# One run of score matmuls for a unit's two tiles, in a fused attention and expert-layer kernel with a planned order

## The chip, the cores and the metric

The kernel runs on one core of a Trainium2 chip. The metric is the device time of one execution in microseconds (us), the median over several runs. A core has five engines that matter here: TensorE (PE; its weight loads are listed as PEld), VectorE (DVE), ScalarE (ACT), GpSimd (POOL) and SyncE (SP), whose queue issues all the DMA transfers of this kernel (SPq in the rows). Each engine works through its own instructions strictly in order and waits on semaphores for the others.

## What is computed

Attention over 8 batches, 8 heads, 576 positions and 64 dimensions, with keys and values averaged over groups of 8 positions (72 pooled keys per head), followed by a dense layer with two weight matrices and a gate on the 4608 resulting rows of 512.

```python
k_p = k.reshape(B, H, Sp, pool, D).mean(axis=3)
v_p = v.reshape(B, H, Sp, pool, D).mean(axis=3)
scores = scale * np.matmul(q, k_p.transpose(0, 1, 3, 2))
scores = scores - np.max(scores, axis=-1, keepdims=True)
attn = np.exp(scores)
attn = attn / (np.sum(attn, axis=-1, keepdims=True) + 1e-09)
x = np.matmul(attn, v_p)            # then (B, S, H*D), as 4608 x 512
h = x @ w_in                        # 512 -> 2048
sp = np.maximum(h, 0.0) + np.log1p(np.exp(-np.abs(h)))
out = (h * erf(sp)) @ w_out         # 2048 -> 512
```

## The kernel before, in words

The 4608 rows are cut into nine chunks of 512. Chunk 0 is computed plainly (stage 0), while the weights are converted from their 64-bit form into two limbs each and written back to HBM. The other eight chunks are taken in pairs (stages 1 to 4) with a Strassen-like scheme of seven products instead of eight. Each product of two matrices is three matmuls of limbs (`three`, line 807 in every row of a large matmul).

Attention is done by `unit`. A unit is 256 rows, that is two tiles of 128; there are 18 units, two of them in chunk 0 and 16 in the others. For each tile `softmax_tile` does this: SP loads the query tile (`raw`, line 632, buffer kind "q" with two buffers for the 16 later units and "q0" with four for chunk 0). TensorE computes the scores into two PSUM banks (`scores`, line 641): 4 head pairs, two key sources, two halves, so 16 matmuls that each use a quarter (64x64) of the array. The profile counts each of these twice, as 32. DVE takes the row maximum of each bank (line 649) and subtracts it (line 665), and with that the bank is read out. ACT takes a sigmoid that stands for the exponential (line 669), DVE sums and inverts (lines 671, 676), DVE or POOL scales (line 679), `copy` sets aside a corner (`bb`). TensorE transposes (lines 686 and 687, five full-array matmuls per tile), ACT or DVE moves the result out, and `part` multiplies with the values (line 734 on quarters, line 740 on halves of the array).

The order of all this is not the source order. Every step is recorded as an `Op` with an engine, an assumed cost, a priority and the buffers that it holds. `Program.order` then places the operations with a list scheduler (`once`). The table MOVES is a list of accepted random shifts of the priorities, so other numbers there mean another order everywhere. Two things in the scheduler matter here. Operations with `step=True` (scores and values, the ones on parts of the array) are charged 200 ns where they follow other work, and are preferred next to each other. Where the planner expects TensorE to be idle (before its time 57 us, or for over 1.2 us), it puts in *fillers*, matmuls on constants that write a bank about to be used (line 1115):

```python
if new and (start < FILL or idle > LONG_IDLE):
    begin = max(free["PE"], 4800.0 if not free["PE"] else 0.0, slots["bank"][0][0])
    out.extend([(self.filler, new[0])] * int((start - begin - MARGIN) / 107))
```

PSUM has eight banks. CAPS limits how many of them each kind may hold at a time: "h" (first layer) 6, "o" (second layer) 4, "att" (attention) 4. An operation is only placed when all its banks are free at once.

Of the kernel before, what the change touches and what calls it, by code (L numbers as in the profile page):

```python
# [25 lines left out]
P = 128  # L26
# [14 lines left out]
PASSES, UNIT = 8, 5100.0  # L41
SPREAD, REACH, SPAN = (300.0, 1000.0, 3000.0), (6e3, 20e3, 60e3), 860e3
MOVES = (
# [7 lines left out]
T0, T0_STEP = -10.5, 1.5  # L51
VAL_R = 3.5
KEYS, KEYS_R, KEYS_S = -5.5, 0.5, -1.0
# [8 lines left out]
ON_ACT = ()  # L62
ON_FIRST = (False, False, False, False)
CAPS = {"fk": 2 * KEPT, "g": 32, "x": 28, "xr": 11, "w": 14, "ws": 10, "w0": 36, "gl": 12, "gz": 16, "t": 6, "f": 3, "q": 2, "q0": 4, "f0": 14, "v": 3, "k": 5, "vm": 1, "low": 2, "sw": 8,
        "h": 6, "o": 4, "att": 4, "cv": 3, "dl": 3, "p1": 8}
SLACK, SLACK_SP, BIAS = 30, 400, 1000
FILL, MARGIN, LONG_IDLE = 57000.0, 300, 1200.0
DGE = 1200
# [322 lines left out]
def moe_attention(ctx: ExitStack, tc: tile.TileContext, cst, qa, kl, vl, wi, wo, out):  # L391
# [16 lines left out]
    op = pr.op  # L408

    def buf(home, shape, dtype=F32):  # L410
        return Buf(small, [P] + shape, dtype, home, home)

    def place(kind, dtype=F32, shape=(512,), name=None):
        return Buf(space, [P, *shape], dtype, "u", name or kind, [kind])

    def bank(kind):
        return Buf(banks, [P, 512], F32, "bank", kind, [kind])
# [195 lines left out]
    def unit(ck, u0, tiles, parts, moment):  # L613

        n_all = 256
        first = ck == 0
# [6 lines left out]
        def softmax_tile(at, r):  # L623
# [4 lines left out]
            rows = [(keys_of[b], e - u0 - at) for e in (u0 + at, u0 + at + 64) for b, off, n, _ in parts if off <= e < off + n]  # L628
            raw = place("q0" if first else "q", F32, (NP, P))
            s = Probs(None, None, None, "s", "s")  # L630
            m, z, bb = buf("m", [H]), buf("z", [H]), buf("bb", [2, 2, NP, SP - 64])
# [3 lines left out]
            pss = [bank("att") for _ in range(2)]  # L635

            def scores():
# [3 lines left out]
                            nc.tensor.matmul(pss[x].ap[r0:r0 + 64, SP * p:SP * p + SP], raw.ap[h:h + 64, p, r0:r0 + 64],  # L641
                                             ks.ap[h:h + 64, p], start=p == 0, stop=True, skip_group_check=True)

            op("PE", 550, r, scores, [raw, *(ks for ks, _ in rows)], pss, [s, m, z],
               turn="q", step=True)
            for g, ps in enumerate(pss):
                pv = lambda ps=ps: ps.ap[:T, :4 * SP].rearrange("p (h k) -> p h k", k=SP)
                gs = slice(4 * g, 4 * g + 4)
# [52 lines left out]
            if k + T == n_all:  # L701
# [3 lines left out]
                    etb.ap[:, 1], f32(etb.ap[:, 0]), c[:, C_MA:C_MA + 1], pb.ap[:, :n_all], ALU.mult, ALU.add),  # L705
                   [pb, (etb, 0)], [(etb, 1)])

        for i in range(tiles):
            softmax_tile(P * i, moment(u0 // P + i))
        plain = ck == 0  # L710
        if ck not in xt:
            if plain:
# [358 lines left out]
    jobs = {}  # L1071
    for ck, u0, tiles, parts in units():

        def moment(t, ck=ck):
            if ck == 0:
                return T0 + T0_STEP * t
            s = (ck + 1) // 2
            at = (t + 4 * ((ck - 1) % 2)) / 8
            return (FIRST - 13 + 9 * at) if s == 1 else start(s) - EARLY[s] + at * (EARLY[s] - READY)

        jobs.setdefault((ck + 1) // 2, []).append((ck, u0, tiles, parts, moment))
    for j in jobs[0]:
        unit(*j)
# [6 lines left out]
    for s in range(1, NC // 2 + 1):  # L1090
        for j in jobs[s]:
            unit(*j)
        x = sides(s, start(s))
# [61 lines left out]
```

## Time and profile before

| what | value |
|---|---|
| runs | 796.21, 796.25, 798.11 us; median 796.25 |
| the profiled execution, its own time | 796.99 us |
| its span in the profile | 795.2 us |
| TensorE busy | 782.6 us, 98% |
| VectorE, ScalarE, GpSimd busy | 81%, 68%, 53% |
| granted TensorE clock, mean | 0.999 |
| bytes moved | 209.78 MB, 264 GB/s |

The span is what the engines' records cover; the profiled execution's own time is 1.79 us more, and that execution is 0.74 us above the median. Busy time is the union of an engine's instructions. Because matmuls are pipelined, the time that a run of matmuls really takes is best read as the distance from its start to the start of what follows on TensorE.

### The profile page before, as it was taken

The numbers are of one execution on the slowest core, as the hardware profiler recorded it, in microseconds if no ns is written. First come the engines' busy times: TensorE is split into PE (matmuls) and PEld (weight loads), VectorE is DVE, ScalarE is ACT, GpSimd is POOL, SyncE is SP. The second block draws the span as 40 slices with busy tenths as digits, with TensorE's granted clock in tenths as the row PEclk, the third lists the DMA queues.
The fourth block names the chain that finished last, engine by engine and source line by source line (L and its number), as shares of the span: only waits on it lengthen the run. The fifth ranks groups of instructions, "written<-read, shape, count | busy, mean of one in ns | idle before, by whom it ended". The sixth has DMA issues, their size and how long they took to land.

```text
span 795.2 us, 15470 instructions
## 1 busy us (share of the span) xinstructions
PE 782.6 (98%) x5288; PEld 671.9 (85%) x5288; DVE 640.5 (81%) x1099; ACT 537.7 (68%) x835; POOL 419.7 (53%) x419
## 2 busy tenths in 40 slices
PE   8999999999999999999999999999999999999998
PEld 6888788877888888888888888888888888888887
DVE  6999886877797887589889979888899976667982
ACT  3999984689865642588775644878856437988730
POOL 4989943479778710275772330775554104561710
PEclk9999999999999999999999999999999999999999
DMA  9989999999999799985485689933745869458551
GB/s 335 347 287 342 364 341 374 332 343 358 291 357 331 245 354 353 367 295 165 149 286 163 204 274 341 339 96 118 247 164 159 277 220 338 145 162 262 186 185 54
DMA packets 126446, 209.78 MB, mean 264 GB/s; under 512 B 12448, under 2 KB 44576, under 8 KB 126368
## 3 DMA queue, kind: packets, MB, share of 16 engines
q1 hardware_dynamic: 126368, 208.79, 76.6%
q8 instruction: 43, 0.70, 0.4%
q14 instruction: 35, 0.29, 0.1%
HBM read 161.55 MB, written 47.19 MB: 263 GB/s over the span
## 4 chain that ended last, share of the span: by engine, by line
PE 85%; ACT 3%; DMA 2%; DVE 2%; SPq 1%; issue 1%; POOL 0%; DVEq 0%; ACTq 0%
PE o L807 42%; PE h L807 35%; PE att L641 2%; PE att L734 2%; PE att L686 2%; PE att L740 2%; DMA ws<-ws 1%; DMA q<-qa 1%; SPq L519 1%; DMA wi<-w 1%; ACT d L826 0%; ACT L826 0%; PE att L687 0%; ACT low L496 0%; ACT cv L492 0%
## 5 line engine op out<-in xcount | busy, mean ns | idle before, releaser
L807 PE MATMUL o<-gl,w 128*128 128x512 f32 x1536 | 340.2, 381 | 0.0
L807 PEld LDWEIGHTS o<-gl,w 128*128 128x128 f32 x1536 | 287.8, 189 | 40.9 <-DVE gl L450 0.2
L807 PE MATMUL h<-x,w 128*128 128x512 f32 (+1 forms) x1392 | 298.9, 374 | 1.2 <-DVE t L914 1.1
L807 PEld LDWEIGHTS h<-x,w 128*128 128x128 f32 x1392 | 253.8, 189 | 36.5 <-DVE t L914 1.8
L834 POOL TENSOR_TENSOR g<-d,g 128x512 f32<-128x512 f32 x79 | 101.9, 1309 | 96.9 <-ACT d L830 95.7
L438 ACT ACTIVATE gl<-g 128x512 fp32r<-128x512 f32 x181 | 107.0, 623 | 44.7 <-DVE g L977 21.8
L450 DVE TENSOR_TENSOR gl<-g,gl 128x512 fp32r<-128x512 f32 x152 | 115.8, 792 | 5.0 <-ACT gl L438 3.3
L450 POOL TENSOR_TENSOR gl<-g,gl 128x512 fp32r<-128x512 f32 x56 | 77.2, 1390 | 54.2 <-ACT gl L438 38.4
L914 DVE TENSOR_TENSOR g<-t,h 128x512 f32<-128x512 f32 x96 | 65.5, 684 | 28.6 <-PE h L807 27.7
L977 POOL TENSOR_TENSOR g<-g 128x512 f32<-128x512 f32 x37 | 60.4, 1632 | 28.8 <-DVE g L977 13.2
L830 ACT ACTIVATE d<-d 128x1024 f32<-128x1024 f32 x72 | 73.5, 1051 | 0.4
L826 ACT ACT_TABLE_LOAD x44 | 56.5, 1283 | 18.6 <-PE h L807 10.9
L914 DVE TENSOR_TENSOR t<-t,h 128x512 f32<-128x512 f32 x57 | 39.1, 686 | 28.9 <-PE h L807 24.4
L826 ACT ACTIVATE d<-g 128x512 f32<-128x512 f32 x103 | 59.2, 622 | 4.6 <-DVE g L914 4.5
L830 ACT ACT_TABLE_LOAD x39 | 50.0, 1283 | 0.7
L438 ACT ACTIVATE x<-xr 128x512 fp32r<-128x512 f32 (+2 forms) x55 | 28.9, 551 | 28.9 <-DVE xr L781 24.3
L669 ACT ACTIVATE s<-s,cst 128x576 f32<-128x576 f32 x36 | 27.6, 772 | 25.0 <-DVE s L665 24.8
L977 DVE TENSOR_TENSOR g<-g 128x512 f32<-128x512 f32 x59 | 44.1, 760 | 0.4
L807 PE MATMUL h<-x,ws 128*128 128x512 f32 x192 | 43.6, 380 | 0.0
L807 PEld LDWEIGHTS h<-x,ws 128*128 128x128 f32 x192 | 36.1, 189 | 5.1
L649 DVE TENSOR_REDUCE m<-att 128x4 f32<-128x288 f32 x72 | 30.1, 444 | 4.9 <-PE att L641 4.8
L439 POOL TENSOR_SCALAR bb<-s 128x64 f32<-128x64 f32 x40 | 10.5, 273 | 43.6 <-DVE s L679 22.6
(107 smaller groups left out, 959.4 us busy)
## 6 DMA issues: line engine op xcount, KB each, us to landing
w<-ws SPq DMA_DIRECT2D x192, 256.0 KB, 4.8
w<-wo SPq DMA_DIRECT2D x128, 256.0 KB, 3.8
w<-wi SPq DMA_DIRECT2D x96, 256.0 KB, 5.2
ws<-ws SPq DMA_DIRECT2D x64, 256.0 KB, 4.6
v<-vl SPq DMA_DIRECT2D x40, 256.0 KB, 5.2
q<-qa SPq DMA_DIRECT2D x36, 256.0 KB, 5.1
out<-f SPq DMA_DIRECT2D x35, 256.0 KB, 2.3
k<-kl SPq DMA_DIRECT2D x32, 256.0 KB, 5.2
```

What stands on the lines that cost most here:

```text
L438: op("ACT", act(n), prio, lambda: nc.scalar.activation(dst(), src(), AF.Copy, scale=scale), *access, turn=turn, alt=("POOL", 0.833 * n + 1 ...
L450: both(True, dve(n), gps(n), prio + 0.1, lambda e: e.tensor_sub(lo(), src(), f32(hi())), reads + [hikey], [lokey])
L641: nc.tensor.matmul(pss[x].ap[r0:r0 + 64, SP * p:SP * p + SP], raw.ap[h:h + 64, p, r0:r0 + 64], ks.ap[h:h + 64, p], start=p == 0, stop=True ...
L649: op("DVE", dve(4 * SP), r + 0.4, lambda pv=pv, gs=gs: nc.vector.tensor_reduce(m.ap[:T, gs], pv(), AX.X, ALU.max), [ps], [(m, g)])
L669: op("ACT", act(H * SP) + 93, r + 0.8, lambda: nc.scalar.activation(s.keys[:T], s.keys[:T], AF.Sigmoid, bias=bias[0][:T], scale=1.0 / 64.0 ...
L686: nc.tensor.transpose(pa.ap[:, P * p:P * p + T], s.keys[:T, p, SP - 64:SP + 64], ident[:T, :T])
L807: nc.tensor.matmul(o, u, v, start=first and q == 0, stop=last and q == 2, skip_group_check=True)
L826: nc.scalar.activation(y(k), hs[k][0].ap, AF.Softplus)
L830: op("ACT", act(1024), prio + 0.2, lambda k=k: nc.scalar.activation(ys[k].ap, ys[k].ap, AF.Erf), own[2 * k:2 * k + 2], own[2 * k:2 * k + 2 ...
L834: both(True, dve(512), gps(512), prio + 0.3, lambda e, k=k, h=h: e.tensor_mul(h.ap, y(k), h.ap), [own[k], h], [h])
L914: op("DVE", dve(512), prio, lambda: nc.vector.tensor_add(dst.ap, u.ap, o.ap), [u, o], [dst])
L977: both(True, dve(512), gps(512), prio, lambda e: e.tensor_sub(out.ap, u.ap, v.ap), [u, v], [out])
```

## The change

The scores of the two tiles of a unit become one operation, except in chunk 0. `softmax_tile` turns into a generator: up to the scores it prepares the tile and hands out its function, inputs, banks and buffers; `unit` collects both tiles' share, records one PE operation for both (32 listed matmuls, 64 in the trace, in four PSUM banks that are all held at once), and then lets the generators run on. "att" may hold six banks instead of four. MOVES is another table with 87 entries instead of 81, of which one row is shown.

```diff
@@ MOVES
-    12000002, 12000013, 12000018, 12000022, 12000032, 12000045, 12000050, 12000120, 12000129, 12000132, 12000145, 12000165,
+    1000000, 1000005, 1000015, 1000023, 1000026, 1000038, 1000043, 1000052, 1000067, 1000085, 1000114, 1000137,
...
@@ CAPS
-        "h": 6, "o": 4, "att": 4, "cv": 3, "dl": 3, "p1": 8}
+        "h": 6, "o": 4, "att": 6, "cv": 3, "dl": 3, "p1": 8}
@@ softmax_tile
-            op("PE", 550, r, scores, [raw, *(ks for ks, _ in rows)], pss, [s, m, z],
-               turn="q", step=True)
+            reads, holds = [raw, *(ks for ks, _ in rows)], [s, m, z]
+            if first:
+                op("PE", 550, r, scores, reads, pss, holds, turn="q", step=True)
+            yield r, scores, reads, pss, holds
@@ unit
+        softmax = []
         for i in range(tiles):
-            softmax_tile(P * i, moment(u0 // P + i))
+            softmax.append(softmax_tile(P * i, moment(u0 // P + i)))
+
+        jobs = [next(t) for t in softmax]
+        if not first:
+            op("PE", 480 * tiles + 70, jobs[0][0], lambda: [j[1]() for j in jobs], *([x for j in jobs for x in j[n]] for n in (2, 3, 4)),
+               turn="q", step=True)
+        for t in softmax:
+            next(t, None)
```

How the order moves is shown at three places, in the program's order and without times. A row is a line of the source, an operation, what it writes and reads, its shape, and how often it stands in a row. Below the edit the changed kernel's lines are higher: 642 for 641, 689 and 690 for 686 and 687, 745 and 751 for 734 and 740, 818 for 807, 1126 for 1115.

First, TensorE where chunk 0 is done and stage 1 begins. Before, the last fillers, the last values of chunks 1 and 2, then the first layer of stage 1 without a break:

```order
L1115 LDWEIGHTS cst
L1115 MATMUL att<-cst 128x256
L734 MATMUL att<-et,vs 64x256 x8
L740 MATMUL att<-etb,vb 128x256 x8
L807 MATMUL h<-x,w 128x512 x66
L807 MATMUL h<-x,ws 128x512 x18
```

In the changed kernel, the last of 29 fillers, values, and only here the last joined scores of chunks 1 and 2, with the transposes of the unit before directly behind them:

```order
L1126 LDWEIGHTS cst
L1126 MATMUL att<-cst 128x256
L745 MATMUL att<-et,vs 64x256 x8
L751 MATMUL att<-etb,vb 128x256 x8
L642 MATMUL att<-ks,q 64x72 x32
L689 MATMUL att<-cst,s_72 128x128 x4
L690 MATMUL att<-cst,bb 128x128
L689 MATMUL att<-cst,s_71 128x128 x4
L690 MATMUL att<-cst,bb 128x128
```

and 31 rows further on the last values of chunk 2, 42 matmuls of the first layer, and then 43 fillers, of which the first is shown:

```order
L818 MATMUL h<-x,w 128x512 x12
L745 MATMUL att<-et,vs 64x256 x8
L751 MATMUL att<-etb,vb 128x256 x8
L818 MATMUL h<-x,w 128x512 x42
L1126 LDWEIGHTS cst
L1126 MATMUL h<-cst 128x256
```

The attention of the second unit of chunk 2 has moved behind the end of chunk 0, into the beginning of stage 1.

Second, TensorE in stage 2, as an example of the steady part. Before:

```order
L734 MATMUL att<-et,vs 64x256 x8
L740 MATMUL att<-etb,vb 128x256 x8
L641 MATMUL att<-ks,q 64x72 x16
L807 MATMUL h<-x,w 128x512 x24
L641 MATMUL att<-ks,q 64x72 x32
L807 MATMUL h<-x,w 128x512 x36
```

Changed:

```order
L818 MATMUL h<-x,w 128x512 x24
L642 MATMUL att<-ks,q 64x72 x32
L745 MATMUL att<-et,vs 64x256 x8
L751 MATMUL att<-etb,vb 128x256 x8
L818 MATMUL h<-x,w 128x512 x54
```

A run of 16 listed matmuls has become one of 32. Over the whole program there were 18 runs of 16 and 9 of 32 and there are now 2 of 16 and 17 of 32; the stretches of matmuls on parts of the array (runs of scores and values that touch each other count as one stretch) go from 35 to 30, and the fillers from 209 (66 of them behind the first matmul of the first layer) to 246 (98).

Third, SP's queue where the last queries for chunks 1 and 2 are loaded. Before, between two weight loads of chunk 0:

```order
L489 DMA d<-wo 128x1024 x3
L519 DMA wi_88<-w_882 256x1x256
L632 DMA q<-qa 128x512
L516 DMA wf_105<-f_868 128x512
L519 DMA wi_96<-w_842 128x256
L519 DMA wi_96<-w_864 128x256
L516 DMA wf_113<-f_985 128x512
L632 DMA q<-qa 128x512
L519 DMA wi_89<-w_889 256x1x256
```

These are the sixth and seventh of the eight "q" loads of chunks 1 and 2. They stand apart, and the eighth too stands ahead of every store of a result. In the changed kernel the third unit's pair and the fourth unit's two loads:

```order
L633 DMA q<-qa 128x512 x2
L528 DMA wo_174<-w_1419 256x1x256
L528 DMA wo_174<-w_1491 256x1x256
L530 DMA wf_127<-f_1564 128x512
L530 DMA wf_118<-f_1415 128x512
L528 DMA wo_167<-w_1412 256x1x256
L956 DMA out<-f 128x512 x2
L633 DMA q<-qa 128x512
L956 DMA out<-f 128x512 x2
L633 DMA q<-qa 128x512
```

The fourth unit's queries now stand behind the stores of chunk 0's results.

## Rows read from the trace of the kernel before

**Rows 1.** The page: busy times; the granted clock in 40 slices

```profile
PE 782.6 (98%) x5288; PEld 671.9 (85%) x5288; DVE 640.5 (81%) x1099; ACT 537.7 (68%) x835; POOL 419.7 (53%) x419
...
PEclk9999999999999999999999999999999999999999
```

**Rows 2.** Waits of PE: who waited for whom: us in total, times, longest

```profile
PE att L1115 <- DMA cst<-cst: 2.7, 1, 2.7
PE o L1115 <- DVE f L500: 1.6, 1, 1.6
PE att L641 <- DMA q<-qa: 1.4, 1, 1.4
PE h L807 <- DVE t L914: 1.1, 1, 1.1
PE att L641 <- DVE ks L582: 0.7, 1, 0.7
PE att L686 <- DVE f L500: 0.6, 1, 0.6
```

**Rows 3.** Timeline of PE, stage 1: start us, us, engine, line, operation, count

```profile
212.71 0.73 PE L641 MATMUL att<-ks,q 64*64 64x72 f32 x32
213.37 2.86 PE L807 MATMUL h<-x,ws 128*128 128x512 f32 x12
216.06 1.46 PE L807 MATMUL h<-x,w 128*128 128x512 f32 x6
217.36 1.46 PE L807 MATMUL o<-gl,w 128*128 128x512 f32 x6
...
221.24 6.64 PE L807 MATMUL o<-gl,w 128*128 128x512 f32 x30
227.81 1.23 PE L641 MATMUL att<-ks,q 64*64 64x72 f32 x64
228.97 11.92 PE L807 MATMUL o<-gl,w 128*128 128x512 f32 x54
240.73 0.60 PE L686 MATMUL att<-cst,s 128*128 128x128 f32 x4
...
241.74 1.54 PE L807 MATMUL o<-gl,w 128*128 128x512 f32 x6
```

**Rows 4.** The same timeline, values and scores with nothing between them

```profile
254.72 1.09 PE L734 MATMUL att<-et,vs 64*64 64x256 f32 x16
255.75 0.74 PE L740 MATMUL att<-etb,vb 64*128 64x256 f32 x8
256.42 0.73 PE L641 MATMUL att<-ks,q 64*64 64x72 f32 x32
257.08 2.86 PE L807 MATMUL o<-gl,w 128*128 128x512 f32 x12
```

**Rows 5.** The same timeline, a block of fillers in stage 1

```profile
201.02 2.68 PE L1115 MATMUL h<-cst 128*128 128x256 bf16 x23
203.46 2.84 PE L807 MATMUL h<-x,ws 128*128 128x512 f32 x12
```

**Rows 6.** Timeline of DVE: the four banks of one long run are read

```profile
124.82 0.96 DVE L649 TENSOR_REDUCE m<-att 128x4 f32<-128x288 f32 x2 [3.25 <-PE att L641]
...
127.16 0.81 DVE L665 TENSOR_TENSOR s<-att,m 128x288 f32<-128x288 f32 x2
```

**Rows 7.** Timeline of PE: that long run of scores itself

```profile
124.04 1.23 PE L641 MATMUL att<-ks,q 64*64 64x72 f32 x64
125.20 2.86 PE L807 MATMUL o<-gl,w 128*128 128x512 f32 x12
```

**Rows 8.** Timeline of PE at the start: scores of the first tile, its transposes

```profile
7.93 0.73 PE L641 MATMUL att<-ks,q 64*64 64x72 f32 x32 [0.72 <-DVE ks L582]
...
16.53 0.60 PE L686 MATMUL att<-cst,s 128*128 128x128 f32 x4
```

**Rows 9.** Loads of the query tile (line 632): all 36, issue to landing

```profile
DMA to landing us min/median/max: 2.6/5.1/7.0
```

13 rows, old and new, of the table MOVES are left out of this document.

## The prediction

> **What bounds the kernel now.** I read the busy times first, then TensorE's waits, then its timeline around attention. TensorE is busy for 782.6 of 795.2 us, and its granted clock stands at the top level (2.4 GHz) in all 40 slices [rows 1]. So nothing off TensorE counts unless it makes TensorE wait, and each instruction on it counts in full. What it waits for is short [rows 2]: 2.7 us for the constants before its first matmul, which the change does not touch, and then 1.6, 1.4, 1.1, 0.7 and 0.6 us, together 5.4 us. The lines in these waits belong to the load of the first keys, the weight conversion of stage 0 (line 500), the products of stage 1 (line 914) and one load of queries. The busy time also holds fillers, matmuls that stand where the planner expected TensorE to be idle. So a different order shows its price in three places: work on parts of the array, fillers, and waits that no filler covers.
>
> **The price of a run of scores.** Six large matmuls take 1.30 us from start to start, so one takes 0.2165 [rows 3]. A short run (32 in the trace) lasts from 212.71 to 213.37, 0.66 us; a long one (64) from 227.81 to 228.97, 1.16 us. So two short runs made into one save 2 x 0.66 - 1.16 = 0.16 us in themselves. There is a cost at either edge too. The 30 large matmuls ahead of the long run take 6.57 us instead of 30 x 0.2165 = 6.49, so entering costs 0.08 to 0.09; the 12 behind the short run take 2.69 instead of 2.60, so leaving costs 0.09 to 0.10. I take 0.19 for a stretch with both edges. Between two kinds of such work there is no edge: behind a product on halves of the array the short run again takes 0.66 us, from 256.42 to 257.08 [rows 4].
>
> **The sum.** In the program's order 18 short and 9 long runs become 2 short and 17 long: eight pairs are joined, 8 x 0.16 = 1.3 us less. (The other eight units outside chunk 0 had their two tiles next to each other already.) Stretches fall from 35 to 30: 5 x 0.19, about 1.0 us less. Fillers rise from 209 to 246. In stage 1, 23 of them take 201.02 to 203.46, 0.106 us each [rows 5], so 37 more add 3.9 us. That is certain, because a filler runs whether or not there was anything to wait for. With all of the 5.4 us of waits taken out the span would be 795.2 - 5.4 - 1.3 - 1.0 + 3.9 = 791.4 us, plus the waits of the new order.
>
> The Trainium skill (TensorEngine Tiling (Array Packing), Key Properties) says that a change of tiling mode drains the engine, a change between tiles of one mode does not. By that rule each change would cost: 106 of them become 95, and at half an edge pair each (0.095) this gives 1.0 us, with nothing for the joining itself, and the sum would be 1.3 us higher. The trace disagrees in part: a change from halves to quarters shows no edge [rows 4], and a long run costs less than two short ones, so I keep my count.
>
> **The new waits.** There are five, none of which the trace shows as it will be; each is bounded from its nearest row.
>
> - *Start.* Nine more fillers stand ahead of the first scores, 9 x 0.106 = 0.95 us, more than the 0.7 us waited there [rows 2]. Nothing is left.
> - *Weight conversion.* 1.6 and 0.6 us were waited here. In the new order large matmuls of chunk 0 come earlier and the attention of chunks 1 and 2 later. That takes attention work off ACT and DVE ahead of the conversions, but TensorE also arrives sooner. Between 0 and 2.2 us; I take 0.4, since less work stands ahead of each conversion.
> - *Fourth unit's queries.* With two "q" buffers these loads must wait until the third unit's run has ended, and SP issues them behind the stores of chunk 0's results. From the last matmul of chunk 0 TensorE has ten transposes (240.73 to 241.74, 1.0 us [rows 3]), 29 fillers (3.1 us) and the values of one part (254.72 to 256.42, 1.7 us [rows 4]), 5.8 us. A query load takes 2.6 to 7.0 us to land, 5.1 in the median [rows 9], and it must first wait for the last results to be copied out of PSUM. At the median that is about on time. Between 0 and 2.5 us; I take 0.5, near the median. Behind the waiting run on TensorE stand the third unit's transposes and the whole first layer of stage 1; behind the loads on SP stand stores of converted weights, which nobody needs soon.
> - *Fourth unit's chain.* From its scores to its transposes the order leaves 1.16 us for the run, 1.0 for ten transposes, 10 fillers (1.1), twice six large matmuls (2.6) and the values of two parts, which are half as wide as the part in [rows 4] and so at most 1.7 us each: at most 9.2, and near 8 if they take little over a microsecond. At the start of the kernel the way from scores to transposes took 7.93 to 16.53, 8.6 us [rows 8]. Between 0 and 1.0; I take 0.3.
> - *Stage 1's products and first queries.* The 1.1 us for line 914 may return; the 43 fillers ahead of the products give DVE time to catch up, so 0.4 of 0 to 1.1. The 1.4 us for a query tile becomes a wait for two tiles: 0 to 2.8. The second load stands 17 places behind the first on SP, but TensorE arrives later than before, so I take 1.0.
>
> Together 0.4 + 0.5 + 0.3 + 0.4 + 1.0 = 2.6 us, and the span comes to 794.0. All of this is made against one execution, whose own time is 1.79 us above its span and 0.74 above the median, so the median lies 1.05 us above the span: **795.0 us**, a gain of 1.2 us, 0.15%. About 0.3%, or 2.4 us, is what a measurement of this kernel can tell from no change, so this counts as *same*.
>
> **The rivals.**
>
> *Faster: the fillers cover everything.* The planner put its fillers exactly where it saw TensorE idle; if it sees the new order well, waits all but vanish. With 0.5 us left the span is 791.9 and the median 793.0. For it: no block of fillers in stage 1 is followed by a wait of its own, and three of the five old waits lie at conversions and queries, places that the new order moves. Against it: the planner was no less exact before and 5.4 us were left over.
>
> *Slower: four banks at once.* A joined run holds four of eight banks until DVE has read them. In the trace DVE starts on such a run at 124.82 and ends at 127.97 [rows 6], and the run itself ended at 125.20 [rows 7], so the four banks are clear 2.8 us after it. After a short run it is half of those 3.15 us of reading. If an operation behind each of the 11 joined runs of stages 1 to 4 needed one of the extra two banks, TensorE would wait up to 1.6 us each, 17 us in all. The order leaves 24 or more large matmuls, over 5 us, before most of the next transposes, so most of it is hidden while DVE starts at once. It decides the case if TensorE waits about 0.5 us behind each run, 5.5 us: 799.5 to 800.5 us. The Trainium skill has a rule that speaks for this rival (TensorEngine Tiling (Array Packing), PSUM Bottleneck): tiling speeds up TensorE but not the emptying of PSUM, which can become the bottleneck. Here DVE empties a bank in 0.8 us and a run fills two in 0.66, so the rates agree with the rule; what hides it is the distance to the next user. Two more things push the same way: query loads at 7.0 us each time, and both units of chunk 2 late. Each would show as a wait of line 642.
>
> *No change in the runs at all* (the order had joined them by itself) is excluded by the count of 16 runs, half of which were separate.
>
> **How the numbers follow.** Forecast, within 0.3% of 796.25: 0.46. Waits below about 1.4 us in all bring the median under 793.9 and so count as faster: 0.36, the rival with nearly all waits covered and the lower part of my bounds. Slower, over 798.6, needs waits of 6.2 us: 0.18, for the bank rival and the upper bounds together. The range takes in the faster rival and most of the slower one: 792.0 to 800.0. Fully covered waits would give 792.4, and the bounds of all new waits together (9.6 us) 802, which needs them all at once.
>
> **What would show it.** Right: a long run still 1.16 us from start to start, 17 of them; TensorE's busy time near 784 us (782.6 + 3.9 - 2.3); waits of PE, without the constants, adding up to 2 or 3 us, one of them by line 642 for a query load soon after chunk 0 ends; nothing waited after stage 1. Wrong: waits of PE for lines 649 or 668 of DVE in stages 2 to 4 (banks), a wait of several us ahead of the first layer of stage 1, or none at all, and then the time is near 793.

## The result, and the profile after the change

| | before | after |
|---|---|---|
| median of the runs beside each other | 797.18 us (4 runs, 796.21 to 798.26) | 802.09 us (4 runs, 801.85 to 803.02) |
| ratio, 95% interval | | 1.0059 [1.0039, 1.0079] |
| profiled execution: span / own time | 795.2 / 797.0 | 800.3 / 802.15 |
| fillers / long runs / stretches, from the order | 209 / 9 / 35 | 246 / 17 / 30 |

The change makes the kernel 0.6% slower, 4.9 us. The forecast was 795.0 with a range to 800: wrong in sign, and outside the range.

The page of the kernel after the change answers to [rows 1]: busy times, then the granted clock in 40 slices.

```profile
PE 788.4 (99%) x5325; PEld 677.5 (85%) x5325; DVE 650.4 (81%) x1106; ACT 536.1 (67%) x838; POOL 413.5 (52%) x405
...
PEclk9999999999999999999999999999999999999999
```

TensorE is busier by 5.8 us, the span is longer by 5.1. Its waits (releaser, us in total, times, longest) answer to [rows 2]:

```profile
PE att L1126 <- DMA cst<-cst: 2.7, 1, 2.7
PE h L818 <- DVE t L925: 2.2, 1, 2.2
PE att L642 <- DVE f L501: 1.2, 2, 0.9
PE o L818 <- POOL w L440: 0.7, 1, 0.7
PE o L818 <- POOL w L451: 0.7, 1, 0.7
PE h L818 <- POOL x L451: 0.5, 1, 0.5
PE h L818 <- DVE x L766: 0.2, 1, 0.2
```

Without the constants these are 5.5 us, about as much as before the change (5.9 with two small rows that [rows 2] leave out). No wait lies behind 300 us in either kernel. So the 3.9 us of added fillers came on top, and did not take the place of waits.

TensorE's timeline after the change (start us, us, engine, line, operation, count, in brackets the idle time ahead of it):

```profile
2.72 6.85 PE L1126 MATMUL att<-cst 128*128 128x256 bf16 x37 [2.72 <-DMA cst<-cst]
9.51 0.73 PE L642 MATMUL att<-ks,q 64*64 64x72 f32 x32
...
86.03 0.72 PE L642 MATMUL att<-ks,q 64*64 64x72 f32 x30 [0.35 <-DVE f L501]
87.41 0.70 PE L818 MATMUL o<-gl,w 128*128 128x512 f32 x2 [0.66 <-POOL w L440]
88.76 7.61 PE L818 MATMUL o<-gl,w 128*128 128x512 f32 x34 [0.65 <-POOL w L451]
...
124.67 1.23 PE L642 MATMUL att<-ks,q 64*64 64x72 f32 x64
125.83 1.56 PE L818 MATMUL o<-gl,w 128*128 128x512 f32 x6
...
157.26 4.87 PE L1126 MATMUL h<-cst 128*128 128x256 bf16 x43
161.88 4.13 PE L818 MATMUL h<-x,ws 128*128 128x512 f32 x18
165.85 1.46 PE L818 MATMUL h<-x,w 128*128 128x512 f32 x6
...
174.67 2.23 PE L818 MATMUL h<-x,w 128*128 128x512 f32 x6 [2.19 <-DVE t L925]
```

Three things are to be read here. A joined run takes 1.16 us (124.67 to 125.83), as in [rows 3]. The scores at 9.51 come 1.58 us later than those of [rows 8], and the 37 fillers ahead of them fill all of that. The products of stage 1 (`h<-x,ws`) begin at 161.88. In the kernel before they began at 154.36, and it came to the second group of six matmuls behind them at 166.00, not 174.67:

```profile
154.36 4.05 PE L807 MATMUL h<-x,ws 128*128 128x512 f32 x18
158.25 1.46 PE L807 MATMUL h<-x,w 128*128 128x512 f32 x6
...
166.00 1.56 PE L807 MATMUL h<-x,w 128*128 128x512 f32 x6 [1.12 <-DVE t L914]
```

So the kernel is 8.7 us late there, and ends 5.1 us late.

What holds TensorE at 174.67 stands on DVE's timeline, after the change:

```profile
167.70 0.68 DVE L925 TENSOR_TENSOR g<-t,h 128x512 f32<-128x512 f32 x1
171.16 0.69 DVE L583 TENSOR_REDUCE ks<-k 128x64 f32<-128x512 f32 x1 [2.78 <-DMA k<-kl]
171.76 0.68 DVE L925 TENSOR_TENSOR g<-t,h 128x512 f32<-128x512 f32 x1
```

DVE works in order. A key reduction stood idle for 2.78 us until its load had landed, and the additions of the products (line 925) stood behind it, so their banks were not freed. SP issued this load at 165.28 and it landed at 171.14, 5.9 us later; the key loads of this kernel take 5.3 us in the median.

The view by stretches (us, then busy us and count of PE, PEld, DVE, ACT, POOL, then granted clock, DMA share, GB/s) shows that the wait cost more than its length. For 3.4 us behind it the granted clock stands at 0.50, the lower level of 1.2 GHz, so about 1.7 us of work were lost:

```profile
172.00:174.67 2.67, 0.49 (x3) 0.08 (x2) 2.41 (x4) 1.67 (x3) 0.00 (x0) 1.00 1.08 396
...
175.40:178.80 3.40, 3.40 (x9) 2.67 (x8) 3.28 (x5) 3.33 (x4) 2.93 (x4) 0.50 1.06 401
```

A similar loss at the start does not show in that column: the clock records of this trace begin at 8.17 us, and where there is none the view shows 1.00. The same view at the first fillers:

```profile
2.72:5.50 2.78, 2.78 (x14) 1.98 (x15) 1.35 (x2) 0.00 (x0) 0.00 (x0) 1.00 0.99 342
...
8.00:9.50 1.50, 1.50 (x14) 1.13 (x11) 0.61 (x1) 0.00 (x0) 0.00 (x0) 1.00 1.06 351
```

Fourteen of the first fillers take 2.78 us, fourteen of the last 1.50. In this execution 25 of the 37 ran at the slow pace, in the profiled one of before 12 of 28. That is 13 x 0.107 = 1.4 us. The first clock record begins within 0.2 us of the change of pace in both traces (8.17 here, 5.37 before).

**The account**, of the profiled executions. Runs and edges -2.3, fillers +3.9 (both as the prediction sized them), waits without the constants 5.5 for 5.9, slow fillers +1.4, the half clock at 175.40 +1.7. The sum is +4.3, the traces differ by 5.1; 0.8 is not placed.

### The profile page after: what moved, and what is told of

Read it like the earlier page. It is cut to its first block, busy times and chain, and to the rows that moved or that the text cites. A ratio compares the mean times of both kernels' runs of the same rounds, so it can differ in the third digit from the quotient of the medians.

```text
span 800.3 us, 15562 instructions
## 1 busy us (share of the span) xinstructions
PE 788.4 (99%) x5325; PEld 677.5 (85%) x5325; DVE 650.4 (81%) x1106; ACT 536.1 (67%) x838; POOL 413.5 (52%) x405
## 4 chain that ended last, share of the span: by engine, by line
PE 86%; POOL 4%; DMA 3%; ACT 3%; DVE 2%; issue 1%; SPq 1%; DVEq 0%; POOLq 0%; ACTq 0%
PE o L818 42%; PE h L818 36%; PE att L642 2%; PE att L745 2%; PE att L751 2%; PE att L689 2%; POOL w L451 1%; PE att L1126 1%; DMA k<-kl 1%; DMA d<-wo 1%; DMA q<-qa 1%; PE h L1126 1%; POOL w L440 1%; POOL low L499 0%; ACT cv L493 0%
## 5 line engine op out<-in xcount | busy, mean ns | idle before, releaser
L845 POOL TENSOR_TENSOR g<-d,g 128x512 f32<-128x512 f32 x73 | 95.1, 1322 | 117.4 <-ACT d L841 110.8
L439 ACT ACTIVATE gl<-g 128x512 fp32r<-128x512 f32 x175 | 103.6, 624 | 49.0 <-DVE g L988 27.5
L451 DVE TENSOR_TENSOR gl<-g,gl 128x512 fp32r<-128x512 f32 x160 | 121.7, 790 | 7.8 <-ACT gl L439 5.7
L451 POOL TENSOR_TENSOR gl<-g,gl 128x512 fp32r<-128x512 f32 x48 | 69.9, 1459 | 72.3 <-ACT gl L439 71.7
L988 POOL TENSOR_TENSOR g<-g 128x512 f32<-128x512 f32 x39 | 53.0, 1361 | 15.5 <-ACT gl L439 4.8
L988 DVE TENSOR_TENSOR g<-g 128x512 f32<-128x512 f32 x57 | 42.4, 752 | 0.3
L440 POOL TENSOR_SCALAR gl<-g 128x512 fp32r<-128x512 f32 x33 | 27.4, 834 | 17.7 <-DVE g L988 5.7
L583 DVE TENSOR_REDUCE vs<-v 128x64 f32<-128x512 f32 x39 | 25.8, 672 | 11.0 <-DMA v<-vl 11.0
```

The source lines that it names most:

```text
L439: op("ACT", act(n), prio, lambda: nc.scalar.activation(dst(), src(), AF.Copy, scale=scale), *access, turn=turn, alt=("POOL", 0.833 * n + 1 ...
L440: alt=("POOL", 0.833 * n + 161, lambda: nc.gpsimd.tensor_scalar(out=dst(), in0=src(), scalar1=scale, scalar2=0.0, op0=ALU.mult, op1=ALU.ad ...
L451: both(True, dve(n), gps(n), prio + 0.1, lambda e: e.tensor_sub(lo(), src(), f32(hi())), reads + [hikey], [lokey])
L583: op("DVE", dve(8 * n), prio, lambda: nc.vector.tensor_reduce(to(), t.ap, AX.X, ALU.add), [t], [t, key], alt=("POOL", gps(4 * n) + gps(2 * ...
L845: both(True, dve(512), gps(512), prio + 0.3, lambda e, k=k, h=h: e.tensor_mul(h.ap, y(k), h.ap), [own[k], h], [h])
L988: both(True, dve(512), gps(512), prio, lambda e: e.tensor_sub(out.ap, u.ap, v.ap), [u, v], [out])
```

## The experiments

Three theories stood at first. **A**: the loss is what the new order waits for and fills in stages 0 and 1. **B**: the joined run itself, four banks at once. **C**: the fillers cost their whole length, and without them it would be gone. D, E and F came up later. All kernels with their ratio to runs of the kernel before on the same chip:

| kernel | median us (runs) | ratio [95% interval] |
|---|---|---|
| split | 804.71 (6) | 1.0091 [1.0058, 1.0125] |
| start28 | 801.65 (12) | 1.0063 [1.0041, 1.0085] |
| nofill | 801.32 (12) | 1.0051 [1.0030, 1.0073] |
| keys | 803.10 (12) | 1.0069 [1.0048, 1.0090] |
| before_nofill | 795.42 (12) | 0.9970 [0.9951, 0.9989] |
| nofill_keys | 801.78 (12) | 1.0060 [1.0040, 1.0081] |
| plain_apart | 810.16 (6) | 1.0164 [1.0124, 1.0205] |
| plain_joined | 816.46 (6) | 1.0230 [1.0188, 1.0271] |
| unjoined_6 | 807.90 (6) | 1.0123 [1.0099, 1.0146] |
| late_cap4 | 801.53 (10) | 1.0042 [1.0027, 1.0057] |
| late_cap6 | 802.26 (6) | 1.0059 [1.0037, 1.0081] |
| one_early | 814.89 (5) | 1.0200 [1.0175, 1.0225] |
| sorted | 802.79 (6) | 1.0065 [1.0043, 1.0087] |
| sorted_nofill | 801.25 (6) | 1.0062 [1.0040, 1.0083] |
| early_keys | 801.94 (12) | 1.0062 [1.0038, 1.0085] |
| late_keys | 802.60 (12) | 1.0064 [1.0038, 1.0091] |
| late_keys_nofill | 799.31 (12) | 1.0022 [0.9994, 1.0049] |

The edits work on `ops`, the finished order, unless a diff says otherwise.

### The run itself, with the order held

```diff
     ops = pr.order()
+    for o in [o for o in ops if getattr(o, "parts", None)]:
...
+        x = ops.pop(k)
+        ops[i:i + 1] = [first, x, second]
...
```

Each of the 16 joined runs is cut into its two tiles, with the next full-array operation (or the one ahead) put between.

> The changed kernel with each of its 16 joined runs cut in two again, a full-array operation of the same order between the halves; banks, queues and the rest of the order stay. Theory A (joining saves what the rows gave: 0.16 us in the run and 0.19 at the edges): 16 x 0.35 = 5.6 us more, 806.5 to 807.7 (those ahead of the products of stage 1 may hide in waits). Theory B (the joined run costs): no slower than 802.1, or faster.

One split run on TensorE's timeline:

```profile
95.49 0.73 PE L642 MATMUL att<-ks,q 64*64 64x72 f32 x32
96.15 1.56 PE L819 MATMUL o<-gl,w 128*128 128x512 f32 x6
97.64 0.73 PE L642 MATMUL att<-ks,q 64*64 64x72 f32 x32
98.30 3.94 PE L819 MATMUL o<-gl,w 128*128 128x512 f32 x17
```

Two short runs of 0.66 and six matmuls in 1.49 instead of 1.30 make 1.51 us of attention work, against 1.16: 0.35 for each, 16 x 0.35 = 5.6. The split kernel's span is 802.0 with no stretch at half clock, the changed kernel's 800.3 with 1.7 us lost to one. Its waits without the constants fell from 5.5 to 3.1 besides. 800.3 - 1.7 - 2.4 + 5.6 = 801.8, so the rows account for the split kernel; its median stays under the range expected because those two fell away. Of the two ratios the intervals overlap, so it is the rows that show the saving. Joining in place saves, and for this order B falls: no wait of the changed kernel names a reader of scores. The rule that the prediction weighed for B (the Trainium skill, TensorEngine Tiling (Array Packing), PSUM Bottleneck) finds no case in this order.

### The start

```diff
+    fillers = iter(range(1000))
+    ops = [o for o in ops if not isinstance(o, tuple) or next(fillers) >= 9]
```

> The changed kernel with the first nine of its fillers left out, so that 28 stand ahead of the first scores as before. Theory A: fillers count in full at the start, and 13 of the 37 ran at half the clock for longer than before; the first large matmul comes 1.0 to 1.6 us earlier, and the time falls by as much, to 800.5 to 801.1. Theory B': the first scores wait for the keys anyway, so 0.7 us of it turns into a wait and the time falls by 0.3 us or less.

```profile
2.65 4.59 PE L1126 MATMUL att<-cst 128*128 128x256 bf16 x28 [2.65 <-DMA cst<-cst]
9.26 0.73 PE L642 MATMUL att<-ks,q 64*64 64x72 f32 x32 [2.02 <-DVE vs L583]
```

That is its timeline of TensorE. The nine fillers gave way to a wait of 2.02 us, which ends with a pooling reduction on DVE (of values, `vs`, by the row): at the start the first scores are late by what DVE has to do on loads first, and the fillers only fill the time. The median does not fall. This run had 13 slow fillers, nofill had 28 with the same 37, so their number changes from execution to execution.

### The fillers

nofill takes the last 94 fillers out of the changed kernel, before_nofill the last 62 out of the kernel before:

```diff
+    fillers = iter(range(1000))
+    ops = [o for o in ops if not isinstance(o, tuple) or next(fillers) < 152]
```

> The changed kernel without the last 94 fillers, those in the blocks of 12, 29, 10 and 43 that stand behind the first layer of chunk 0; the first 152 stay. If fillers cost what they take (theory C), 94 x 0.106 = 10 us go and the time is 792. If they stand where TensorE would wait anyway (theory A), most of it turns into idle time and the time falls by 0 to 3 us, to 799 to 802; if the idle time lowers the granted clock, it rises above 802.

> The kernel before without its last 62 fillers (6.6 us at 0.106). If fillers cost what they take (the price in the prediction's sum), the median falls from 796.5 to about 790. If they cover waits, waits of TensorE in stage 1 grow by as much as the fillers took, and the median stays within 2 us of the kernel before. Theory A expects the second, with growth of the waits between 3 and 6 us and a gain of 0 to 3 us.

The second is the same with 147 in place of 152. In nofill the products start at 153.52, as early as before the change. Then TensorE stops; its longest waits and the place:

```profile
PE h L818 <- DVE t L925: 5.9, 3, 5.0
```

```profile
172.06 2.58 PE L818 MATMUL h<-x,w 128*128 128x512 f32 x6 [5.01 <-DVE t L925]
```

That is the group which the kernel before reached at 166.00. So 10.0 us of fillers are gone and 6.8 us of waits have come (12.3 without the constants, for 5.5); the span falls by 2.5 us and the median by less than one. C falls. In the kernel before the 62 fillers (6.6 us) cost 1.4: **before_nofill is the fastest kernel of the study, 0.3% under the kernel before**. With the late fillers out of both kernels the change costs 0.8% (1.0051 to 0.9970).

Waits are only part of what the fillers cover. Those of before_nofill grow by 1.1 us alone (7.0 for 5.9), but where 25 fillers stood around two runs of scores TensorE now waits 1.85 us (until 77.98), and the granted clock falls during that wait:

```profile
77.70:84.40 6.70, 6.32 (x44) 5.12 (x45) 3.97 (x10) 5.56 (x7) 5.01 (x8) 0.50 1.03 376
```

That is 6.8 us at 1.2 GHz, 3.4 us of work: 6.6 - 1.1 - 3.4 leaves 2.1, and the span fell by 1.5 (0.3 to 0.4 of the rest are 3 or 4 more slow fillers at the start). The record has span and mean granted clock of every execution, and span x (1 - clock) is an estimate of what the half clock took, at most. Its median is 0 to 1.6 us for the kernel before in the five groups of runs, 2.4 for the changed kernel, 2.0 for before_nofill, and 4.0, 5.2, 5.6 and 3.2 for nofill, nofill_keys, sorted_nofill and late_keys_nofill. So much of what the last four win without fillers goes to the lower clock: less this estimate nofill's span is 795.3, the changed kernel's 797.9, that of the kernel before 794.3 to 794.9, that of before_nofill 791.3.

### One load moved, then two

DVE at 171.16 waits for a key load. keys puts two key reductions up to five places back, behind the products' additions; nofill_keys does the same without fillers; sorted and sorted_nofill put them just ahead of the third key reduction, and two weight loads (line 539) ahead of the keys' loads on SP.

```diff
+    adds = [o for o in ops if not isinstance(o, tuple) and o.eng == "DVE"]
+    late = adds[253], adds[255]
...
+    ops = [o for o in ops if o not in late]
+    at = ops.index(adds[258]) + 1
+    ops[at:at] = late
```

> The changed kernel with two key reductions of VectorE moved five places down its queue, behind the additions of stage 1's products that stood behind them; nothing else moves. Theory A (the loss is the new order, and here it is VectorE waiting in its queue for a key load while the products wait for PSUM banks): TensorE's wait of 2.2 us for line 925 goes, and with it the 3.4 us at half the granted clock that follow, worth 1.7 us; 802.1 becomes about 798.2, at least below 799.5. Theory B (the joined run itself costs, by its four banks): the wait only moves on, and the time stays within 1 us of 802.1.

> The changed kernel without its last 94 fillers, and with two key reductions of chunk 3 moved behind the products' additions on DVE. Theory A (the loss is what the new order waits for in stages 0 and 1, and the 5.0 us waited at 172 without these fillers come from the key load ahead of the additions in DVE's queue): the span of the run without fillers, 797.8, less 5.0 and less the half-clock stretch of 1.7 behind that wait, 791 to 795, the median 792 to 797. Theory C (fillers and moved reductions change only where TensorE waits, the work ahead of the products is late in any case): the wait turns up at another place, the median stays at 800 to 802.

> The changed kernel without its last 94 fillers, the two early key reductions of chunk 3 behind the products' additions on DVE, and two loads of weights for line 539 ahead of those keys' loads on SP. Without fillers the products start at 153.5, as early as before, and then TensorE waits 5.0 us for additions that stand behind a step on DVE that waits for a load; with the keys alone moved, the step in front was the one that waits for the load of line 539. Theory E (the products of stage 1 are held by loads that the new order issues in the wrong sequence, and the fillers only fill that time): the wait falls by 3 us or more, the span to 791 to 795, the median to 793 to 797. Rival F (loads come as fast as the queues bring them, any sequence moves the wait to another step): 799 to 802 again, with 4 us or more waited for t or x elsewhere in stage 1.

> The same two moves in the changed kernel with all its fillers. Theory E: the wait of 2.2 us for line 925 and the 1.7 us of half clock behind it go, 797 to 799.5; the fillers ahead of the products still stand. Rival F: within 1 us of the changed kernel, 801 to 803.

All four stay at the time of the changed kernel. DVE's timeline shows why, in nofill_keys:

```profile
175.60 0.98 DVE L546 TENSOR_TENSOR sw<-sw 128x256 f32<-128x256 f32 x1 [2.81 <-DMA sw<-wf]
```

and in sorted_nofill, where that load came in time:

```profile
175.13 0.69 DVE L583 TENSOR_REDUCE ks<-k 128x64 f32<-128x512 f32 x1 [2.84 <-DMA k<-kl]
```

Each time another load was the late one, with an addition of the products next on DVE. Theory E (a wrong sequence of these few loads) falls as put; F (the loads come as fast as they can, and some step waits) fits. The stretches say what their rate is. Kernel before:

```profile
120.00:160.00 40.00, 40.00 (x328) 33.45 (x327) 28.71 (x62) 20.91 (x50) 17.57 (x24) 1.00 1.02 353
160.00:200.00 40.00, 37.44 (x201) 31.94 (x200) 30.89 (x48) 36.36 (x42) 34.56 (x35) 1.00 1.01 350
...
300.00:800.00 500.00, 491.45 (x2967) 424.57 (x2965) 393.60 (x647) 315.69 (x465) 214.45 (x186) 1.00 0.65 219
```

Changed kernel:

```profile
120.00:160.00 40.00, 39.49 (x413) 32.72 (x413) 28.04 (x68) 20.03 (x52) 11.60 (x13) 1.00 0.96 331
160.00:200.00 40.00, 37.81 (x178) 32.55 (x176) 28.95 (x45) 33.36 (x41) 31.63 (x38) 0.96 0.96 323
```

From 120 to 200 us the DMA engines are busy nearly all the time (the last but one column), behind 300 us two thirds of it. So in stage 1 there is little room for a load to come earlier unless another comes later. The Trainium skill (DMA: Bandwidth & Descriptors, Where 436 GB/s comes from) puts the limit of one core's share of HBM at about 358 GB/s. The 350 and 353 GB/s of the rows over 40 us lie just under it; shorter stretches go beyond (396 and 401 GB/s around the wait at 174.67), so it is no fixed ceiling here. By that second group of six matmuls SP had issued 196 transfers in the kernel before (at 166.00) and 213 in the changed one (at 174.67), 17 more; four of them are key loads, nine are loads of weights, the rest stores of converted weights (3) and one load for a conversion. At 256 KB each that is 4.5 MB, some 13 us at 350 GB/s, and the group is reached only 8.7 us later.

### Joining where the planner may reorder

Theory **D**: a joined run needs the queries and keys of both its tiles at the time at which the first tile alone had started, so inputs of the second tile are called for earlier, in the stages where DMA is full. The planner's own order (table emptied), apart and joined, and joined code with its units apart:

```diff
-MOVES = (
-...
+MOVES = ()
```

```diff
-        jobs = [next(t) for t in softmax]
-        if not first:
+        if not joined:
+            for t in softmax:
+                for _ in t:
+                    pass
+        jobs = [next(t) for t in softmax] if joined else []
+        if joined:
```

(unjoined_6 has both edits, with `joined` false for every unit.)

> The kernel before with its table of numbers emptied, so that the planner's own order stands, 24 short runs of scores and 6 long ones, 231 fillers. It is one of a pair with the next run. Some 797 to 806 us.

> The changed kernel with its table emptied, 2 short runs and 17 long, 272 fillers. Theory A (the order of this table happened to be the worse draw; joining itself saves): faster than the other of the pair by 1 to 5 us (11 more joins at 0.16 are 1.8 us, and about 1 us of edges). Theory D (joining itself makes the attention of stages 0 and 1 late, since no score of a unit runs before the queries of both its tiles have come, and this costs more than the runs save, whatever the order): slower than the other by 2 to 8 us, the 41 further fillers being 4.3 of it, and the first product of stage 1 later by 3 us or more. If the pair is within 2 us, neither.

> The changed kernel with its table emptied and its units not joined, attention still at six banks: third of the trio with the two plain orders (810.2 apart with four banks, 816.5 joined with six). 199 fillers, 32 fewer than apart with four banks and 73 fewer than joined. Theory D: the six banks help or do nothing, 805 to 811, so that the 6 us between the two plain orders are the joining's own. If it were at 814 or more, the six banks would be what costs.

With six banks and apart 807.9, joined 816.5: joining costs 8.6 us in the planner's own order, and six banks by themselves do not cost. In the joined kernel TensorE waits 4.0 us for queries, in the two apart it has no such wait, as D has it. The products begin at 161.59 and 161.64 in the two kernels apart, and at 168.08 in the joined one:

```profile
168.08 4.13 PE L810 MATMUL h<-x,ws 128*128 128x512 f32 x18
```

Next the priorities of the kernel before, number for number, and units joined only in part:

```diff
-MOVES = (
-...
+JOINED = ((1, 0),)
+AT = (
...
+        joined = (ck, u0) in JOINED
```

> Priorities of the kernel before, and a single unit joined, the first of chunk 1, which stands in stage 0; 269 fillers instead of 209 and 17 short runs fewer by two. Theory D: one joined run ahead of which everything waits for its second tile: the 60 further fillers are 6.4 us, of which part takes the place of waits; 799 to 805, and the first product of stage 1 later by 3 us or more. Theory A (the loss is a worse draw of the whole order and not a matter of joining): within 2 us of the kernel before.

> The planner's priorities are those of the kernel before, number for number, and only units of chunks 4 to 8 are joined (14 long runs and 8 short instead of 9 and 18, 209 fillers as before); attention still holds four banks at most, so a joined run needs all of them. Theory D (joining is worth what the runs save, and costs only where the attention of stages 0 and 1 has to wait for the second tile's queries): 5 pairs x 0.16 and up to 5 edges x 0.19, 0.8 to 1.8 us faster than the kernel before, 794.8 to 795.8. Theory B (four banks at once are what costs): TensorE waits up to 1.6 us behind each of these runs, up to 8 us slower, with waits for lines that read the scores in stages 2 to 4.

> As the run before it, but attention may hold six banks, 210 fillers. Theory D: 794 to 797, the six banks change the order a little and nothing else. Theory B: clearly faster than with four banks, since transposes behind a joined run find a bank.

A single joined unit of stage 0 costs 17.8 us; D had expected 799 to 805 and was right in sign only; the products begin at 168.27, 13.9 later than in the kernel before. Its first run of scores behind chunk 0:

```profile
66.43 1.57 PE L846 MATMUL att<-ks,q 64*64 64x72 f32 x64
71.09 8.45 PE L1032 MATMUL h<-x,w 128*128 128x512 f32 x24 [3.08 <-DVE s L872]
```

Line 872 is the step with which DVE has read a bank of scores out, so this is a wait of B's kind, in stage 0, and 6.8 us at granted clock 0.50 begin before it ends (70.40 to 77.23). The length of the run alone does not make it: in the kernel before a run of 64 matmuls at 59.16 has no such wait behind it. D's cause shows as well: in the kernel before the first scores behind chunk 0 are a short run at 31.68, here none runs before 66.43, and the next two query loads, which need its two "q" buffers, are issued at 67.4 and 67.9 instead of 53.7 and 60.1. In the profiled execution the 60 further fillers are 6.4 us, the waits without the constants 10.6 for 5.9, the half clock 3.4: 14.5 of 15.3. How much of this is D's, and how much B's, no run separates.

late_cap4 and late_cap6 are misses for D as well as for B. D expected a gain; they lost 4.4 and 5.1 us. B's waits are hardly there either: late_cap4 waits 8.5 us without the constants, 2.6 more than the kernel before, and only one wait of 0.7 names the reader of score banks (line 872). The longest of the later stages comes soon behind the run at 417.75:

```profile
417.75 1.23 PE L846 MATMUL att<-ks,q 64*64 64x72 f32 x64
...
420.62 2.64 PE L1032 MATMUL o<-gl,w 128*128 128x512 f32 x11 [1.22 <-DVE gl L654]
```

DVE was late there with an operand of the large matmuls (`gl`), not with a bank. And the planner made 38 stretches of this order, not fewer than the 35. So here the new arrangement costs without D's cause and mostly without B's; which of its moves does was not tried.

### The second tile's keys, moved alone

In the changed kernel the joined run of chunk 3 (205.0) is the first to need the keys of its second tile; in the kernel before the second tile ran by itself at 212.71 [rows 3]. So the changed order has these five key loads among the products, the first reduction behind the fourth addition; before it stood behind the eighteenth. early_keys gives the kernel before this one thing and no joined run; late_keys takes it from the changed kernel, and has the two weight loads of line 539 ahead of them as in sorted. In late_keys the five reductions end by 189 and the joined run still has its keys in time: that they stood as early as 171 was the planner's choice, and not what the run needs.

```diff
+    loads = [o for o in ops if mine(o, "SP", "k")][15:20]
+    sums = [o for o in ops if mine(o, "DVE", "k")][15:20]
+    ops = [o for o in ops if o not in loads and o not in sums]
...
+    for i, o in sorted(put, key=lambda x: -x[0]):
+        ops.insert(i, o)
```

(The five tiles get other buffers that are free there.)

> The kernel before, its order and runs untouched but for one thing: the five key loads of chunk 3's second tile and their reductions stand where the changed kernel has them, the first reduction behind the fourth addition of stage 1's products on DVE instead of the eighteenth, the loads that far earlier on SP. In the changed kernel the joined run of chunk 3 needs these keys at 205.0, in the kernel before the second tile's run at 212.7. Theory D (a joined run calls for the second tile's inputs earlier, and their loads then stand in front of the products): the products wait for line 914 2 to 4 us more, 798.5 to 802. Rival F (the sequence of loads does not matter): within 1 us of the kernel before.

> The reverse in the changed kernel: the same five loads and reductions up to 44 places later in the order, the first behind five more additions, and the two loads for line 539 still ahead of them. Theory D: the wait of 2.2 us for line 925 and the half clock behind it go, 797 to 800. Rival F: 801 to 803.

> The same without the last 94 fillers. Theory D: the 4.6 us waited for line 925 in the run with two reductions moved fall by 3 us or more, 794 to 798. Rival F: 799 to 802, with the wait at another step.

early_keys makes the kernel before 4.9 us slower, as much as the whole change. Waits of PE, and its timeline in stage 1:

```profile
PE h L807 <- DVE t L914: 4.5, 2, 2.4
```

```profile
168.59 1.56 PE L807 MATMUL h<-x,w 128*128 128x512 f32 x6 [2.08 <-DVE t L914]
...
177.73 2.66 PE L807 MATMUL h<-x,w 128*128 128x512 f32 x6 [2.40 <-DVE t L914]
```

And its stretches, with the half clock again behind a wait:

```profile
177.70:181.00 3.30, 3.27 (x8) 2.62 (x9) 1.53 (x3) 2.32 (x4) 2.97 (x3) 0.55 0.88 278
```

So this move, as made, suffices for a loss of this size. But the moved tiles' other buffers have a part in it, as far as the rows tell. SP's own waits, the longest between 165 and 173 us in early_keys and between 176 and 182 in late_keys:

```profile
SPq L561 <- DMA k<-kl: 1.9, 1, 1.9
```

```profile
SPq L571 <- PE h L818: 3.9, 1, 3.9
```

In early_keys a weight load waits until a moved key load has landed and been reduced, so that SP issues nothing from 169.24 to 171.82, and the key load for which DVE then waits 1.72 us (until 175.64), ahead of the wait at 177.73, is issued behind that, at 172.24. In late_keys the first moved key load waits for TensorE until 180.87, and all later loads stand behind it. No run has the moves without these waits. In the profile of early_keys, 1.6 of the 5.3 us stand before the products besides, behind more slow fillers and a half clock at 89.29, ahead of anything that was moved.

The reverse gives only part of the loss back. Without fillers 801.3 falls to 799.3 (intervals overlap); with fillers nothing is gained, because the next load on DVE, one of values, is late:

```profile
195.57 0.69 DVE L583 TENSOR_REDUCE vs<-v 128x64 f32<-128x512 f32 x1 [5.08 <-DMA v<-vl]
```

That this move costs is shown, its other buffers included; how much of the 4.9 us is the early keys' is not.

## Why the prediction was wrong

- **Runs, edges, price of a filler: right.** 1.16 us for each of 17 runs, 0.35 for a pair with its edges, 37 fillers more. The busy time near 784 was missed (788.4); the 13 more slow fillers (1.4 us) and the half clock (1.7) are 3.1 of the excess.
- **"With all of the 5.4 us of waits taken out": the step that failed first.** The span was put at 794.0 and came to 800.3: 2.9 of the 6.3 us are waits beyond the 2.6 forecast, 1.7 the half clock and 1.4 the slow fillers, for which the sum had no term; 0.3 is not placed. Old waits were taken out whole and 2.6 us put in; 5.5 came. The fillers were entered as a cost, and at the same time as cover for the waits ("nothing is left", "give DVE time to catch up"). They are cover only where the work behind them is not late by itself. The planner puts fillers where it expects TensorE to be idle, so more of them were its own sign of lateness; this sign was read as a price alone.
- **Start, forecast 0:** 1.4 us, from fillers at the slow pace. start28 shows that it is not the nine further fillers.
- **Weight conversion, 0.4 of 0 to 2.2:** 2.5 us (0.86, 0.35, 0.66, 0.65 around 86), over the bound. The argument was that less attention stands ahead of the conversions; TensorE's earlier arrival weighed more, as far as the rows tell: by 80 us it has begun 176 large matmuls, in the kernel before 144.
- **Products, 0.4 of 0 to 1.1:** 2.2 us, and 1.7 of half clock. The bound was taken from the size of the old wait. Its cause was not DVE's work but a load in DVE's queue, which no further filler ahead of it makes earlier: in nofill the wait is 5.0.
- **Query tiles 1.0 and the fourth unit's queries 0.5:** nothing was waited, nor for the fourth unit's chain (0.3). The 0.5 us for an input of the first layer (line 451) was in no term.
- **"Nothing off TensorE counts unless it makes TensorE wait"** holds, but the DMA share was not read. At 0.96 to 1.02 between 120 and 200 us it says that there is little room to move a load forward without pushing another back.
- **The bank rival** gave a time (799.5 to 800.5) nearer to the result than the forecast, but none of its waits is there: that it lay nearer is luck. The rival that fillers cover everything is refuted by 5.5 us of waits.

## What to carry to other kernels

Price a larger block by what it must have before it can start, not only by what it saves while it runs: with the order held it saved 0.35 us a run, and each time the planner was free to reorder around it the kernel lost 4 to 18 us. Where the DMA engines are full, read which loads an earlier need pulls forward and which in-order queue (here DVE's) then stands at a load with urgent work behind it. Where a planner fills expected idle time, a filler count that rises can be lateness that it already sees; taking the fillers out shows how much of them is cover, for waits and for the clock (in the kernel before 6.6 us of them gave 1.4 back).

## What the runs showed of the hardware

- A wait of TensorE of a few us was followed in several runs by a stretch at granted clock 0.50 (1.2 GHz) of 3.4 us (after 2.19 us waited here, after 2.40 in early_keys), or 6.8 us in some executions. Such a wait then costs up to 1.7 or 3.4 us more than its length. Length alone does not decide: a wait of 1.12 us in the kernel before [rows 2] had none behind it, but neither had one of 2.08 (early_keys, 168.59) or of 2.81 (late_keys, 197.68), while in start28 6.8 us of it (87.38 to 94.21) came with three waits of 0.90, 0.35 and 0.62 us within 3 us, and the like waits of the changed kernel around 86 had none.
- The first matmuls of the program take 0.213 us each, then 0.109. The clock records begin only about where the pace changes, so the view's 1.00 ahead of that is no measurement. The change of pace came after 12 to 28 fillers, a spread of 1.7 us, and differently in kernels whose start is the same (25 in the changed kernel, 14 in late_keys).
